# Norming block 1 of sequence 0 by the common path, and moving three loads of x behind a later norm

## The chip, the cores and the metric

One core of one Trainium2 chip. The metric is the device time of one execution in microseconds (us): before the change the median of 3 runs is 859.71 us (859.6 to 859.87). The engines are TensorE (PE; its weight loads are shown apart as PEld), VectorE (DVE), ScalarE (ACT), GpSimd (POOL) and SyncE (SP). SP only issues transfers, and GpSimd issues some as well.

## The reference

Eight sequences of 3008 rows and 256 columns are filtered along the rows in the frequency domain. Each row of the result is then normed, and goes through a gated feed-forward layer of width 1536.

```python
X = np.fft.rfft(x, axis=1)
Y = X * (filt_r + 1j * filt_i)[None, :, :]
y = np.fft.irfft(Y, n=x.shape[1], axis=1)          # per sequence
rms = np.sqrt(np.mean(y * y, axis=-1, keepdims=True) + 1e-06)
xn = y / rms * rms_g
g = xn @ w_gate
out = (g * (1 / (1 + np.exp(-g))) * (xn @ w_val)) @ w_out
```

## The kernel before, in words

**The mixing.** 3008 is 47 times 64, so the transform is made in two steps of matmuls for each sequence. Step a (`a_unit`) takes x from a tile of `x_load` (384 KB, four for each sequence, issued by GpSimd, float32 in HBM to float16 in SBUF) and its result goes to HBM by `z_store`. `t2_load` brings it back in another layout, four loads for each sequence. Step b (`b_unit`, or `b_soft`) is a matmul, followed by the product with the filter (`s_part`, `add_unit`). A transposing transfer (`yt_load`), step bi (`bi_unit`) and four transposing transfers (`t4_load`) follow. All transfers but the loads of x and of the weights are issued by SP.

**The norm.** The output rows come in six blocks of four tiles (m = 0 to 5) for each sequence. `norm_plan` gives a block to the common path: `n_unit` twice (one matmul of 512 columns into the PSUM bank "mx", and its copy to the float32 tile y by ACT), `sq_unit` twice (two squares with their sums on ACT), `stat_unit` (u and rho, the mean and its power of -1/2, on GpSimd), `xt_unit` (y times rho on GpSimd) and `tr_unit` (a transposing transfer on SP, from xt to xn). Block 0 of sequence 0 has its own path, `first_norm`. Block 1 of sequence 0 has another one: `n_first` (eight matmuls of 128 columns, two squares and two copies on ACT), `q_unit` (eight matmuls that sum the squares, u on DVE, rho on GpSimd), `scale_split` (two small operations on DVE) and `scale_apply` (eight matmuls that spread rho over the partitions, and two products on DVE that write xn). It uses no transfer.

**The feed-forward layer.** `items` lists 576 slots (b, m, jt): eight sequences, six blocks, twelve slices of the width. In slot i the program issues `gv` (four matmuls of 512 columns, lines 553, into the banks pg and pv, two buffers each; then Silu on ACT, L557, and the product on DVE, L558), then the planned steps of that slot in the order of a list, then `down` for slot i - 2 (four matmuls of 256 columns, L578). Slot 12 is the first that reads xn of block 1, slot 24 the first that reads xn of block 2.

**What sets the order.** Each engine runs its instructions in the order of the program. `fit` finds a slot for a step by a load that it counts for each engine and bank ("A" ACT, "V" DVE, "M" and "B" the banks "mx" and "mb"), and `at` puts the step into the plan of that slot. `XAT` holds the earliest slots of the loads of x: (6, 8, 11, 29) for sequence 2. Transfers that SP issues run on one queue, in the profile q1, and those of GpSimd on another, q0. Both are served by the core's 16 DMA engines.

Around the change the plan of before is: slot 2 the first `z_store` of sequence 1; slot 3 `n_first`; slot 5 `q_unit` (behind `down`); slot 7 `scale_split`; slot 9 `scale_apply`; slots 5 to 11 the eight `a_unit` of sequence 1 that are left, all with their copies on ACT; slots 6, 8 and 11 three loads of x of sequence 2; slots 7, 9 and 12 the other three `z_store`; slots 12 to 20 the norm of block 2 (`stat_unit` in 16, `xt_unit` in 17, `tr_unit` in 20); slots 15, 16, 17 and 25 the `t2_load` of sequence 1; slot 19 its first `b_unit`.

Of the kernel before, what the change touches and what calls it, by code (L numbers as in the profile page):

```python
# [10 lines left out]
FP32 = mybir.dt.float32  # L11
FP16 = mybir.dt.float16
AXT = mybir.ActivationFunctionType
ALU = mybir.AluOpType
# [6 lines left out]
P = 128  # L21
D = 256
B = 8
# [9 lines left out]
Y_SCALE = N * S_INV_B * S_INV_A  # L33
XC = 6
# [67 lines left out]
def kernel(  # L102
# [11 lines left out]
    nc = tc.nc  # L114
# [17 lines left out]
    xtp = ctx.enter_context(tc.tile_pool(name="xtp", bufs=2))  # L132
    up = ctx.enter_context(tc.tile_pool(name="up", bufs=2))
    xnp = ctx.enter_context(tc.tile_pool(name="xnp", bufs=4))
    hp = ctx.enter_context(tc.tile_pool(name="hp", bufs=4))
    op = ctx.enter_context(tc.tile_pool(name="op", bufs=2))
# [4 lines left out]
    psB = ctx.enter_context(tc.tile_pool(name="psB", bufs=1, space=bass.MemoryType.PSUM))  # L141

    tab = glob.tile([P, 5 * P], FP16)
    wa, wai, ident = (tab[:, ts(i, P)] for i in range(3))
# [13 lines left out]
    ones = glob.tile([P, 1], FP16)  # L158
    epsb = glob.tile([P, 1], FP32)
    warm = glob.tile([P, 4], FP32)  # L160
    mhalf = glob.tile([P, 4], FP32)
    seen = glob.tile([P, 4], FP16)

    st = {b: {"x": {}, "t1": {}, "t2": {}, "s": {}, "yt": {}, "t4": {}, "y": {}, "sq": {},
              "u": {}, "xn": {}} for b in range(B)}
# [4 lines left out]
    def y_tile():  # L170
        t = stg.tile([P, 2, 4, 256], FP32, tag="stg", name="y")
        return t.rearrange("p a b c -> p (a b c)")[:, 0:1024].rearrange("p (a e) -> p a e", a=2)
# [16 lines left out]
    def bank(i, name):  # L189
        pool, tag = ((psM, "mx"), (psG, "pg"), (psV, "pv"), (psB, "mb"), (psO, "po0"))[i]  # L190
        return pool.tile([P, 512], FP32, tag=tag, name=name)

    def copy(eng, out, in_, scale=None):
        if eng == "A":
            nc.scalar.activation(out=out, in_=in_, func=AXT.Copy, **({} if scale is None else {"scale": scale}))  # L195
        elif scale is None:
            nc.vector.tensor_copy(out=out, in_=in_)
        else:
            nc.vector.tensor_scalar(out=out, in0=in_, scalar1=scale, scalar2=None, op0=ALU.mult)
# [277 lines left out]
        nc.scalar.activation(out=warm, in_=mhalf, func=AXT.Silu)  # L477
        st[0]["xn"][0] = xn

    def n_first(m):  # L480
        y = y_tile()
        sq = xtp.tile([P, 4, D], FP16, tag="xt", name="sq").rearrange("p (a e) d -> p a (e d)", a=2)
        psn = [bank((0, 3)[h], "psn") for h in range(2)]
        for h in range(2):
            for q in (2 * h, 2 * h + 1):
                n1p = 4 * m + q
                src = st[0]["t4"][n1p // XC][:, n1p % XC]
                for dh in range(2):
                    nc.tensor.matmul(psn[h][:, ts(2 * (q % 2) + dh, P)], src[:, ds(dh * P, P)], wai,
                                     start=True, stop=True)  # L490
        for h in range(2):
            nc.scalar.activation(out=sq[:, h, :], in_=psn[h], func=AXT.Square)
        for h in range(2):
            copy("A", y[:, h, :], psn[h])
        st[0]["sq"][m] = sq
        st[0]["y"][m] = y

    def q_unit(m):
        sq = st[0]["sq"].pop(m)
        ps = psB.tile([P, 4], FP32, tag="mb", name="psq")  # L500
        for q in range(4):
            for dh in range(2):
                nc.tensor.matmul(ps[:, q:q + 1], sq[:, q // 2, ts(2 * (q % 2) + dh, P)], ones,
                                 start=(dh == 0), stop=(dh == 1))
        u = up.tile([P, 4], FP32, tag="u", name="u")
        rho = up.tile([P, 4], FP32, tag="rho", name="rho")
        nc.vector.tensor_scalar(out=u, in0=ps, scalar1=1.0 / D, scalar2=1e-6 * Y_SCALE * Y_SCALE,
                                op0=ALU.mult, op1=ALU.add)
        nc.gpsimd.tensor_tensor(out=rho, in0=u, in1=mhalf, op=ALU.pow)
        st[0]["u"][m] = rho  # L510

    def scale_split(m):
        rho = st[0]["u"].pop(m)
        hl = up.tile([P, 2, 4], FP16, tag="hl", name="hl")
        nc.vector.tensor_copy(out=hl[:, 0, :], in_=rho)
        nc.vector.tensor_tensor(out=hl[:, 1, :], in0=rho, in1=hl[:, 0, :], op=ALU.subtract)
        st[0]["u"][m] = hl

    def scale_apply(m, bk):
        hl = st[0]["u"].pop(m)  # L520
        y = st[0]["y"].pop(m)
        ps = bank(bk, "psr")
        for q in range(4):
            for e in range(2):
                nc.tensor.matmul(ps[:, ts(q, P)], hl[:, e, q:q + 1].to_broadcast([P, P]), ident,
                                 start=(e == 0), stop=(e == 1))
        xn = xnp.tile([P, 4, 2, P], FP16, tag="xn", name="xn")
        pv = ps.rearrange("p (q t) -> p q t", q=4)
        for h in range(2):
            nc.vector.tensor_tensor(out=xn[:, 2 * h:2 * h + 2],  # L530
                                    in0=pv[:, 2 * h:2 * h + 2].unsqueeze(2).to_broadcast([P, 2, 2, P]),
                                    in1=y[:, h, :].rearrange("p (q e t) -> p q e t", q=2, e=2), op=ALU.mult)
        st[0]["xn"][m] = xn

    LAST = (B - 1, 5)
    hh_of = {}
    po_of = {}
# [92 lines left out]
    with tc.manual_schedule():  # L630
# [48 lines left out]
        todo = [(i, f, dh) for i in range(2) for f in range(2) for dh in range(2)][:7] + [(2, 0, 0)]  # L679
# [58 lines left out]
        a_out(1, 2, "V", ahead[0])  # L738

        items = [(b, m, jt) for b in range(B) for m in range(6) for jt in range(JT)]  # L740
        plan, late = {}, {}
        front = (sq_unit, s_part, add_unit)
        load = {r: [0.0] * (len(items) + 99) for r in "MBAV"}
        room = {"A": 0.8, "V": 0.7}
# [2 lines left out]
            load["V"][i] = 0.68  # L747

        def at(slot, fn, *a):
            todo = (late if fn == q_unit else plan).setdefault(slot, [])  # L750
            if fn in front:
                todo.insert(0, (fn, a))
            else:
                todo.append((fn, a))
# [20 lines left out]
        def norm_plan(b, m, slots, r):  # L775
            for i in range(2):
                s = fit(slots[i], ("M", 0, 1), ("A", 0, 0.6), ("A", 1, 0.82))
                at(s, n_unit, b, m, i)
                at(s + 1, sq_unit, b, m, i)
            for d, fn in zip(r, (stat_unit, xt_unit, tr_unit)):  # L780
                at(s + d, fn, b, m)
            assert s + r[-1] + 1 < 72 * b + 12 * m

        def a_plan(b, slots):
            for i in range(4 * (b == 1), 12):
                opts = []
                for k in "MB":
                    opts.append((k, "A", ((k, 0, 1), ("A", 0, 0.6))))
                    opts.append((k, "V", ((k, 0, 1), (k, 1, 1), ("V", 0, 0.68))))
                k, e, need = min(opts, key=lambda o: fit(slots[i], *o[2], keep=False))  # L790
                s = fit(slots[i], *need)
                at(s, a_unit, b, i, e, 0 if k == 'M' else 3)
                if i % 3 == 2:
                    at(s + 1, z_store, b, i // 3)
                    if b + 1 < B:
                        at(max(s + 2, XAT.get(b + 1, (0,) * 4)[i // 3]), x_load, b + 1, i // 3)
            return s + 1
# [20 lines left out]
                        at(last, bi_unit, b, u)  # L818
            return last

        XAT = {2: (6, 8, 11, 29), 3: (47, 51, 79, 88), 4: (112, 122, 132, 142)}
        at(0, a_out, 1, 3, "A", ahead[1])
        at(2, z_store, 1, 0)
        at(XAT[2][0], x_load, 2, 0)
        at(3, n_first, 1)
        at(5, q_unit, 1)
        at(7, scale_split, 1)
        at(9, scale_apply, 1, 3)
        load["M"][3] = load["M"][4] = 1
        load["B"][3] = load["B"][4] = load["B"][5] = load["B"][9] = load["B"][10] = 1  # L830
        load["A"][3] = load["A"][4] = 1.2
        for m, n_at in ((2, 12), (3, 20), (4, 31), (5, 42)):
            norm_plan(0, m, (n_at, n_at + 2), (2, 3, 6))
        for b in range(1, B):
            t = (b - 1) * 72
# [43 lines left out]
        for i in range(len(items) + 4):  # L879
            for fn, a in early.pop(i, ()):  # L880
                fn(*a)
            if i < len(items):
                gv(*items[i])
            for fn, a in plan.pop(i, ()):
                fn(*a)
            if 2 <= i < len(items) + 2:
                b, m, jt = items[i - 2]
                if jt == 1 and i > JT:
                    down(b, m, 0)
                if jt or i < JT:  # L890
                    down(b, m, jt)
                if items[i - 2][2] == JT - 1:
                    stores[i + 1] = items[i - 2][:2]
            for fn, a in late.pop(i, ()):
                fn(*a)
            if i in stores:
                o_store(*stores[i])
        assert not plan and not late and not early


# [28 lines left out]
```

## Time and profile before

| what | value |
|---|---|
| median of 3 runs | 859.71 us |
| the profiled execution, its own time | 859.65 us |
| its span, first to last instruction | 857.9 us |
| what lies around the span | 1.75 us |
| granted TensorE clock | 1.000 |
| PE busy | 849.2 us (99%), 6139 matmuls |
| DVE busy | 557.2 us (65%) |
| ACT busy | 612.5 us (71%) |
| POOL busy | 298.1 us (35%) |
| DMA packets of q1 (SP), of q0 (GpSimd) | 189464 (85.52 MB), 8544 (21.24 MB) |

The page's busy time of PE is not work at its peak, since matmuls are pipelined. What a stretch costs is read from the distance between the starts of the same matmul in successive slots. The slots begin at 43.20 us of the span (slot 0) and the last matmul ends at 853.6 us.

### The profile page before, as it was taken

How to read it: one execution, taken by the hardware profiler on the slowest of the kernel's cores; microseconds unless marked ns; L12 is line 12 of the kernel's file. 1: busy time of each engine (PE TensorE's matmuls, PEld its weight loads, DVE VectorE, ACT ScalarE, POOL GpSimd, SP SyncE). 2: the span in 40 equal slices, each digit the busy share in tenths (PEclk: the TensorE clock that was granted, in tenths of full speed). 3: DMA queues.
4: the chain of work that ended last, by engine and by line, in shares of the span. 5: the costliest groups of instructions: out<-in, count | busy, mean ns of one | idle time of the engine just before them, and what ended most of it. 6: DMA issues, size and time to landing. Idle time of an engine off the chain costs nothing.

```text
span 857.9 us, 17015 instructions
## 1 busy us (share of the span) xinstructions
PE 849.2 (99%) x6139; PEld 532.5 (62%) x6139; DVE 557.2 (65%) x926; ACT 612.5 (71%) x1338; POOL 298.1 (35%) x346
## 2 busy tenths in 40 slices
PE   8999999999999999999999999999999999999997
PEld 6766666666666666666666666666666666665655
DVE  5857755776666666666666676767666665555554
ACT  4987887786687757887578865887567765777444
POOL 5725732543154413443044430444123430132000
PEclk9999999999999999999999999999999999999999
DMA  9995878756975566746747658434574431521101
GB/s 282 273 206 126 152 169 168 148 123 137 186 138 140 108 142 114 158 117 129 152 122 115 120 108 185 105 81 113 122 126 93 98 69 42 123 56 50 63 25 50
DMA packets 198237, 107.98 MB, mean 126 GB/s; under 512 B 158566, under 2 KB 182520, under 8 KB 198152
## 3 DMA queue, kind: packets, MB, share of 16 engines
q1 hardware_dynamic: 189464, 85.52, 44.9%
q0 software_dynamic: 8544, 21.24, 12.9%
q8 instruction: 48, 0.79, 0.4%
q14 instruction: 37, 0.30, 0.1%
q10 hardware_dynamic: 144, 0.13, 0.0%
HBM read 45.78 MB, written 35.65 MB: 95 GB/s over the span
## 4 chain that ended last, share of the span: by engine, by line
PE 97%; DMA 1%; DVE 0%; ACT 0%; POOL 0%; issue 0%; DVEq 0%; POOLq 0%
PE po L578 29%; PE pg L553 28%; PE pv L553 28%; PE psb L248 3%; PE psi L292 3%; PE psn L321 2%; PE psa L204 2%; DMA fs<-in_filt_i_dram 1%; PE psy L425 1%; PE psf L396 1%; PE pst L374 0%; POOL xc L186 0%; DVE s L238 0%; ACT ff L195 0%; ACT sq L455 0%
## 5 line engine op out<-in xcount | busy, mean ns | idle before, releaser
L558 DVE TENSOR_TENSOR hh<-pv,sg 128x512 f16<-128x512 f32 (+1 forms) x577 | 391.6, 679 | 283.4 <-ACT sg L557 220.5
L557 ACT ACTIVATE sg<-pg 128x512 f16<-128x512 f32 (+1 forms) x577 | 337.5, 585 | 215.2 <-PE pg L553 211.4
L553 PE MATMUL pg<-xn,wg 128*128 128x512 f16 (+2 forms) x1156 | 337.9, 374 | 0.0
L553 PE MATMUL pv<-xn,wv 128*128 128x512 f16 (+2 forms) x1156 | 337.8, 374 | 0.0
L578 PE MATMUL po<-wo,hh 128*128 128x256 f16 x2256 | 332.7, 272 | 0.0
L578 PEld LDWEIGHTS <-hh 128*128 128x128 f16 x2256 | 213.4, 98 | 105.2
L275 POOL TENSOR_TENSOR ss<-s,s 128x384 f16<-128x384 f16 x112 | 102.0, 912 | 267.4 <-DVE s L241 239.8
L553 PEld LDWEIGHTS <-wv 128*128 128x128 f16 x1156 | 113.0, 98 | 130.6 <-issue 0.2
L553 PEld LDWEIGHTS <-wg 128*128 128x128 f16 x1156 | 111.5, 98 | 16.9 <-issue 0.2
L347 POOL TENSOR_TENSOR xt<-y,rho 128x1024 f16<-128x1024 f32 (+1 forms) x46 | 85.4, 1857 | 2.9
L329 ACT ACTIVATE junk<-y 128x256 f16<-128x256 f32 x180 | 74.3, 413 | 2.8
L238 DVE TENSOR_TENSOR s<-psb,ff 128x384 f16<-128x384 f32 x124 | 67.8, 548 | 0.7 <-ACT ff L195 0.6
L241 DVE TENSOR_TENSOR s<-psb,ff 128x384 f16<-128x384 f32 x124 | 67.7, 547 | 0.0
L195 ACT ACTIVATE uu<-psi 128x384 f16<-128x384 f32 (+1 forms) x127 | 61.8, 487 | 1.1
L195 ACT ACTIVATE y<-psn 128x512 f32<-128x512 f32 (+1 forms) x95 | 55.7, 588 | 4.2
L292 PEld LDWEIGHTS <-yt 96*128 96x128 f16 x512 | 35.5, 97 | 26.2 <-issue 0.2
L339 POOL TENSOR_TENSOR rho<-u,mhalf 128x4 f32<-128x4 f32 (+1 forms) x46 | 46.5, 1011 | 3.8
L337 POOL TENSOR_SCALAR u<-ss 128x4 f32<-128x4 f32 (+1 forms) x46 | 8.9, 194 | 106.4 <-ACT junk L329 105.4
L195 ACT ACTIVATE t<-psa 128x512 f16<-128x512 f32 x70 | 41.4, 595 | 2.8 <-PE psa L204 1.4
L292 PE MATMUL psi<-wi,yt 96*128 96x96 f16 x512 | 42.9, 205 | 0.0
L248 PE MATMUL psb<-wb,t 96*128 96x96 f16 x480 | 40.0, 206 | 0.0
L248 PEld LDWEIGHTS <-t 96*128 96x128 f16 x480 | 29.3, 97 | 10.7 <-issue 0.2
(102 smaller groups left out, 364.2 us busy)
## 6 DMA issues: line engine op xcount, KB each, us to landing
out_dram<-o SPq DMA_DIRECT2D x40, 512.0 KB, 3.5
xc<-in_x_dram POOLq DMA_DIRECT2D x31, 384.0 KB, 6.1
z_tmp<-t SPq DMA_DIRECT2D x28, 384.0 KB, 2.7
t<-z_tmp SPq DMA_DIRECT2D x28, 384.0 KB, 6.0
out_dram<-o SPq DMA_DIRECT2D x7, 384.0 KB, 2.7
fs<-in_filt_i_dram POOLq DMA_DIRECT2D x3, 512.0 KB, 10.8
fs<-in_filt_r_dram POOLq DMA_DIRECT2D x3, 512.0 KB, 11.3
ws<-in_moe_w_gate_dram POOLq DMA_DIRECT2D x3, 512.0 KB, 10.0
```

The lines of the kernel that those rows point to most:

```text
L195: nc.scalar.activation(out=out, in_=in_, func=AXT.Copy, **({} if scale is None else {"scale": scale}))
L238: eng.tensor_tensor(out=o, in0=ps, in1=f1, op=ALU.mult)
L241: eng.tensor_tensor(out=o, in0=ps[:, :, ::-1, :], in1=f2, op=ALU.mult)
L248: nc.tensor.matmul(ps[:, ts(k, KR)], st[b]["t2"][kk // KC][:, kk % KC, ds(dh * P, P)], wb[0:KR, kk, :], start=True, stop=True)
L275: nc.gpsimd.tensor_tensor(out=ss3[g % 3][:, :, dh, 0:KR], in0=s[0], in1=s[1], op=ALU.add)
L292: nc.tensor.matmul(ps[:, k, :], yt[0:KR, k, dh, :], wi[0:KR, 4 * g + k, :], start=True, stop=True)
L329: nc.scalar.activation(out=junk, in_=y[:, i, ts(u, D)], func=AXT.Square, accum_out=ss[:, 2 * i + u:2 * i + u + 1])
L347: nc.gpsimd.tensor_tensor(out=xt[:, 0:n, :], in0=y.rearrange("p a (u d) -> p (a u) d", u=2)[:, 0:n, :], in1=rho[:, 0:n].unsqueeze(2).to_br ...
L553: nc.tensor.matmul(ps[:, (r0 - q0) * P:(r1 - q0) * P], wt[:, dt_, ts(jt, P)], xn[:, r0:r1, dt_, :], start=(dt_ == 0), stop=(dt_ == 1))
L557: nc.scalar.activation(out=sg[:, c], in_=pg[:, 0:w], func=AXT.Silu)
L558: nc.vector.tensor_tensor(out=hh[:, c], in0=pv[:, 0:w], in1=sg[:, c], op=ALU.mult)
L578: nc.tensor.matmul(po[q - 1][:, 0, :] if own else po[q // 2][:, q % 2, :], hh_of[(b, m, j)][:, ts(q, P)], wo[:, j, :], start=(j == 0 and ( ...
```

## The change

Block 1 of sequence 0 goes to the common path, with `n_unit` in slots 2 and 3, `stat_unit` in slot 5, `xt_unit` in slot 6 and `tr_unit` in slot 8. Its own functions are removed. `fit` then places the steps a of sequence 1 otherwise: unit 4 in slot 4 with its copy on DVE, and one unit in each of the slots 5 to 11, with copies on ACT. The second `z_store` of sequence 1 is put into slot 9 (before: 7). The three loads of x move from the slots 6, 8 and 11 to 17, 18 and 20. In GpSimd's order the first one stands between `stat_unit` and `xt_unit` of block 2, the other two directly behind `xt_unit` of block 2. In SP's order `tr_unit` of block 1 stands between the first and the second `z_store`. From slot 21 on both plans are the same, step for step.

```diff
-    def n_first(m):
-        y = y_tile()
-        sq = xtp.tile([P, 4, D], FP16, tag="xt", name="sq").rearrange("p (a e) d -> p a (e d)", a=2)
...
-    def q_unit(m):
...
-    def scale_split(m):
...
-    def scale_apply(m, bk):
...
-        plan, late = {}, {}
+        plan = {}
...
-            todo = (late if fn == q_unit else plan).setdefault(slot, [])
+            todo = plan.setdefault(slot, [])
...
-                    at(s + 1, z_store, b, i // 3)
+                    at(9 if (b, i) == (1, 5) else s + 1, z_store, b, i // 3)
...
-        XAT = {2: (6, 8, 11, 29), 3: (47, 51, 79, 88), 4: (112, 122, 132, 142)}
+        XAT = {2: (17, 18, 20, 29), 3: (47, 51, 79, 88), 4: (112, 122, 132, 142)}
         at(0, a_out, 1, 3, "A", ahead[1])
         at(2, z_store, 1, 0)
         at(XAT[2][0], x_load, 2, 0)
-        at(3, n_first, 1)
-        at(5, q_unit, 1)
-        at(7, scale_split, 1)
-        at(9, scale_apply, 1, 3)
-        load["M"][3] = load["M"][4] = 1
-        load["B"][3] = load["B"][4] = load["B"][5] = load["B"][9] = load["B"][10] = 1
-        load["A"][3] = load["A"][4] = 1.2
+        norm_plan(0, 1, (2, 3), (2, 3, 5))
         for m, n_at in ((2, 12), (3, 20), (4, 31), (5, 42)):
             norm_plan(0, m, (n_at, n_at + 2), (2, 3, 6))
...
-            for fn, a in late.pop(i, ()):
-                fn(*a)
```

More of the change, by code (lines that the diff above doesn't have):

```diff
@@ L478, in first_norm @@
         st[0]["xn"][0] = xn
-    def n_first(m):
-        y = y_tile()
-        sq = xtp.tile([P, 4, D], FP16, tag="xt", name="sq").rearrange("p (a e) d -> p a (e d)", a=2)
[L483 to L496, printed above, removed]
@@ L498, in q_unit @@
-    def q_unit(m):
[L499 to L510, printed above, removed]
@@ L512, in scale_split @@
-    def scale_split(m):
[L513 to L517, printed above, removed]
-    def scale_apply(m, bk):
[L520 to L533, printed above, removed]
@@ L893 @@
                     stores[i + 1] = items[i - 2][:2]
-            for fn, a in late.pop(i, ()):
-                fn(*a)
             if i in stores:
                 o_store(*stores[i])
-        assert not plan and not late and not early
+        assert not plan and not early
 _INS = ['x', 'filt_r', 'filt_i', 'moe_w_gate', 'moe_w_val', 'moe_w_out', 'moe_rms_g']
```

## The prediction

> **What bounds the kernel now.** I read the page first, then the chain, then the timeline of slots 0 to 26, then the DMA windows.
>
> ```profile
> PE 849.2 (99%) x6139; PEld 532.5 (62%) x6139; DVE 557.2 (65%) x926; ACT 612.5 (71%) x1338; POOL 298.1 (35%) x346
> PE 97%; DMA 1%; DVE 0%; ACT 0%; POOL 0%; issue 0%; DVEq 0%; POOLq 0%
> ```
>
> The chain that ended last is TensorE nearly everywhere. In the table by stages TensorE is busy without a break from 60 us on, and its waits add up to a few us, all before slot 0. So a matmul that goes is a gain, and any wait of TensorE is a loss that nothing later gives back.
>
> **Matmuls removed and added.** Distances between the starts of successive pg pairs (TensorE in the timeline) give the price of a step:
>
> ```profile
> 46.44 0.59 PE L553 MATMUL pg<-xn,wg 128*128 128x512 f16 x2
> ...
> 47.30 0.61 PE L489 MATMUL psn<-tab,t 128*128 128x128 f16 x8
> ...
> 49.48 0.59 PE L553 MATMUL pg<-xn,wg 128*128 128x512 f16 x2
> ```
>
> Slot 4 starts at 48.18 and has no extra step: 49.48 - 48.18 = 1.30 is a plain slot. Slot 3 with `n_first` takes 48.18 - 46.44 = 1.74, so `n_first` costs 0.44. Slot 7 with one `a_unit` takes 1.52 (52.93 to 54.45), so 0.22 for one matmul of 512. Slot 5 with `a_unit` and `q_unit` takes 1.72: `q_unit` 0.20. Slot 9 with `a_unit` and `scale_apply` takes 1.96 (55.96 to 57.92): 0.44. Removed: 0.44 + 0.20 + 0.44 = 1.08. Added: two matmuls of `n_unit`, 0.22 each as in slot 12 (60.95 to 62.47, 1.52): 0.44. The eight `a_unit` of slots 5 to 11 are still eight. **Sum: -0.64 us**, 0.07% of the run. What else decides is whether something new makes TensorE wait.
>
> **Block 1's own path, slots 2 to 12.** ACT loses two squares and two copies (1.08 + 1.09) and one `a_unit` copy (0.60, now 0.69 on DVE, which loses five operations of block 1). It gains two copies (0.60) and two `sq_unit`, which take 0.94 each where they stand elsewhere (63.60 to 64.54). Followed in ACT's order: copy at 46.4, Silu of slot 3 at 47.3, copy at 47.9, squares at 48.5, Silu of slot 4 at 49.45, squares until 51.05, Silu of slot 5 until 51.5. The pg buffer of slot 5 is wanted again at 52.7, that of slot 4 at 51.2 (free at 50.0), so the backlog costs TensorE nothing; if it grew by 1.2 us, it would cost what is above that. GpSimd then does as for block 2 (below): 3.4 us from the end of the squares to the end of xt, so 54.45, and SP issues the transfer there. At that moment the load of x issued at 46.98 has just landed (54.8), no other is queued, since the three of sequence 2 have gone, and the first `z_store` lands at 55.1. Transposing transfers beside stores alone took 3.1 to 4.8 us, so xn lands at 57.5 to 59.3; slot 12 starts at 60.95 - 0.64 = 60.3. Hidden, with 1 us to spare at least. The z stores queued on SP behind this wait go out at about 55.8 in place of 53.1, and the last still leaves near 60.7; their first reader, the `t2_load` behind the store of the output, issues at 65.4. Hidden too.
>
> **The moved loads, slots 17 to 24.** From here I use the clock of before; TensorE, GpSimd and SP all come 0.64 earlier together. GpSimd:
>
> ```profile
> 67.61 0.19 POOL L337 TENSOR_SCALAR u<-ss 128x4 f32<-128x4 f32 x1 [11.04 <-ACT junk L329]
> 67.90 1.04 POOL L339 TENSOR_TENSOR rho<-u,mhalf 128x4 f32<-128x4 f32 x1
> 69.02 1.89 POOL L347 TENSOR_TENSOR xt<-y,rho 128x1024 f16<-128x1024 f32 x1
> ```
>
> SP, and the matmul of slot 24 that needs the xn of this xt:
>
> ```profile
> 66.06 2.25 SPq L228 DMA_DIRECT2D t<-z_tmp  x3
> 70.94 1.26 SPq L356 DMA_TRANSPOSE xn<-xt  x1
> ```
>
> ```profile
> 78.11 0.59 PE L553 MATMUL pg<-xn,wg 128*128 128x512 f16 x2
> ```
>
> In before, three loads of t are on q1 when the transpose is issued at 70.94; it lands 3.6 us later, at 74.55, with 3.5 us to spare. After the change GpSimd issues the first load of x at 68.95 (the end of rho), which takes 0.6 us of GpSimd, so xt ends 0.6 later, at 71.5. There the transpose is issued, and the other two loads in the same 1.2 us. `add_unit`, next on GpSimd, waits for DVE until 73.4 anyway. So three loads of x (q0) meet two loads of t and the transpose (q1), on the same 16 engines. How q0 and q1 share is seen where a load of x met a transpose, at 390 to 391 us:
>
> ```profile
> q0 software_dynamic: 59, 0.18, 93.4%
> q1 hardware_dynamic: 58, 0.01, 11.2%
> ```
>
> The columns are packets, MB and share of the engines. One for one by packets: 3072 bytes of x for each 256 of the transpose. So the transpose hardly moves until the load is through. That load and that transpose, issued within 0.1 us, landed after
>
> ```profile
> xc<-in_x_dram POOLq DMA_DIRECT2D x1, 384.0 KB, 5.2
> xn<-xt SPq DMA_TRANSPOSE x1, 5.9
> ```
>
> [...]
>
> Since q1 is in order and the transpose is its last, it lands when all that work is done. Terms: one load of x alone takes 4.8 us to landing (issued at 90.74), start-up included. Each further one adds 128 packets at 91 in 1.5 us (93.0 to 94.5): 2.1. A load that is issued at 68.95 shows its first packet some 1.3 us later, as that of 90.74 did, so at 70.3. From there on before still had on q1
>
> ```profile
> q1 hardware_dynamic: 2280, 0.87, 98.9%
> ```
>
> of which 1024 are the transpose's, 64 completions, and about 1190 are of t. The last go at 2103 in 4.0 us (68.5 to 72.5), so 2.3; the transpose's at 912 in 1.0 us (270 to 271), so 1.1. Landing: 68.95 + 4.8 + 2 x 2.1 + 2.3 + 1.1 = **81.35**. The same sum for collisions in before comes out at 393.2 (load of 387.29; measured 393.3), 271.5 (265.63; 271.6), 179.9 (172.97, with a store of 1.1; 180.2), 472.7 (466.77; 473.9) and 124.4 (115.31, two loads and a store; 125.8): 0.1 to 1.4 too early, median 0.3. I take 81.6. Slot 24 waits from 78.1 to 81.6: **+3.5 us**. The bounds: 80.6 if the 24 t packets per engine that go between those of x are free (0.7 less), 83 with the largest miss: a wait of 2.5 to 5.
>
> The first load of t, needed by slot 19's `b_unit` at 71.14 and landed at 70.73, has its last packets at 69.8, 0.5 before those of x. Should x catch it, part of the wait moves to slot 19, and the sum stays. The second is read behind slot 24's wait, the third in slot 30; x itself in slot 29, at 85.4. After the wait both plans are equal, and TensorE alone sets the pace.
>
> **Forecast.** 859.65 - 0.64 + 3.5 = 862.5 for an execution like the profiled one; the median of the runs shown lies 0.06 above it, so **862.6**. Its own range is 861.6 to 864.1 (waits of 2.5 to 5).
>
> **Rivals.**
>
> *B, not slower: the queues share engine time, not packets.* Then q1's 3.4 us of work from 70.3 on, after a start-up of 0.8, take twice as long at most: 70.3 + 0.8 + 6.8 + 0.5 for landing = 78.4, a wait of 0.3. It decides at a landing of 78.1. The time is 859.71 - 0.64 + 0.3 = 859.4, or 859.1 without a wait. For it: packets of t (512 bytes) beside x are in no row. Against it: 59 to 58. Chance 0.14.
>
> *C, between them:* the start-up of x doesn't stop q1, or x comes later, and the wait is 0.5 to 2.3: 859.6 to 861.4. Against it: 387 to 389 us, where q1 fell from some 400 packets in half a us to none. Chance 0.10.
>
> *D, the clock falls in the wait.* The kernel's first ten fills (L433, from 1.45 us) take 4.0 us, four later ones 1.0: a cold TensorE runs at about half rate. A wait of 3.5 us is longer than any gap of TensorE in before since the first matmul (0.8). If it brings that state back for 3 to 4 us, 1.7 to 2 more are lost: 864.3 to 864.6, and up to 866 with a long wait. [...] Chance 0.09.
>
> *E, block 1 is late as well.* Its transpose would have to take the 7.1 us of the row at 466.77: landing at 61.6, slot 12 waits 1.3, 863.9. Against it: no load of x is beside it. Chance 0.07.
>
> *The change doesn't do what it says:* the first load does stand behind the statistics of block 2, but ahead of its xt; that is what I priced.
>
> **Chances.** The forecast's case has 0.60. Without B the range would hold about 0.75, so it reaches down to B and leaves out most of D: 859.0 to 864.6. Some 0.2% (1.7 us) is what a measurement here can tell from no change. Faster by more than that needs a gain that no row has: 0.01. Within it are B and C: 0.23. Slower: 0.76.
>
> **What would show it.** In the profile after: psq, psr and `hl` gone and slots 3 to 9 shorter (else the -0.64 is wrong); a wait of TensorE at L553's successor in slot 24, by a DMA xn<-xt, of some 3.5 us; that transpose at about 10 us to landing; x loads of q0 one for one with q1 between 69.7 and 77; none of TensorE in slot 12. If the transpose of block 2 lands in under 6.5 us, the sharing was read wrongly, and the time is near 859.1.

## The result and the profile after

After the change the median is 862.77 us (861.18 to 863.05, 8 executions), before it 859.75 us (859.48 to 860.35, 8 executions). The ratio is 1.003, with a 95% interval of 1.0019 to 1.0041: slower by 3.0 us. The prediction was 862.6, in a range of 859.0 to 864.6.

The 8 executions lie on two levels, and each has its mean granted clock of TensorE (1.000 is full speed): 861.18, 861.32 and 861.88 us at 1.000, and five from 862.71 to 863.05 at 0.997 or 0.998. The profiled execution is on the lower level (861.32 us, span 859.5 us). So two things need an answer: where 861.32 comes from, and what adds some 1.5 us in most executions.

The lines behind the functions of block 1, which are gone, have moved by 55: L498 is the old L553 (`gv`), L523 the old L578 (`down`). The page of after has, for busy time and chain:

```profile
PE 849.1 (99%) x6117; PEld 531.7 (62%) x6117; DVE 556.4 (65%) x922; ACT 612.9 (71%) x1343; POOL 299.9 (35%) x348
PE 96%; DMA 2%; POOL 1%; DVE 0%; ACT 0%; issue 0%; DVEq 0%; POOLq 0%
```

There are 22 matmuls less, and a share of the chain has gone from TensorE to transfers and GpSimd. TensorE's waits in after (us in total, times, longest) begin with one that before does not have:

```profile
PE pg L498 <- DMA xn<-xt: 2.2, 1, 2.2
```

The timeline of TensorE in after, slots 3 and 4 and the start of slot 12, then the start and the end of slot 23 and slot 24:

```profile
46.60 0.59 PE L498 MATMUL pg<-xn,wg 128*128 128x512 f16 x2
...
47.47 0.38 PE L321 MATMUL psn<-t,tab 128*128 128x512 f16 x1
...
48.12 0.59 PE L498 MATMUL pg<-xn,wg 128*128 128x512 f16 x2
...
60.25 0.59 PE L498 MATMUL pg<-xn,wg 128*128 128x512 f16 x2
```

```profile
75.76 0.59 PE L498 MATMUL pg<-xn,wg 128*128 128x512 f16 x2
...
76.96 0.60 PE L523 MATMUL po<-wo,hh 128*128 128x256 f16 x4
79.73 0.59 PE L498 MATMUL pg<-xn,wg 128*128 128x512 f16 x2 [2.17 <-DMA xn<-xt]
```

In before, the slots 12 and 23 start here:

```profile
60.95 0.59 PE L553 MATMUL pg<-xn,wg 128*128 128x512 f16 x2
...
76.47 0.59 PE L553 MATMUL pg<-xn,wg 128*128 128x512 f16 x2
```

Slot 3 takes 1.52 in place of 1.74. Slot 12 starts at 60.25 in place of 60.95, of which 0.05 was there at slot 0 already: 0.65 saved. Slot 23 takes 3.97 us (75.76 to 79.73) in place of 1.64 (76.47 to 78.11): 2.33 lost. Then -0.05 - 0.65 + 2.33 = +1.63, and the spans differ by 859.5 - 857.9 = 1.6. Behind slot 24 the matmuls gain another 0.1 and the end of the program takes 0.15 longer; nothing else in the profiled execution differs.

GpSimd and SP in after, around the norm of block 2:

```profile
67.18 1.01 POOL L339 TENSOR_TENSOR rho<-u,mhalf 128x4 f32<-128x4 f32 x1
68.15 0.64 POOL L186 DMA_DIRECT2D xc<-in_x_dram  x1
68.81 1.91 POOL L347 TENSOR_TENSOR xt<-y,rho 128x1024 f16<-128x1024 f32 x1
70.65 1.24 POOL L186 DMA_DIRECT2D xc<-in_x_dram  x2
```

```profile
65.35 2.21 SPq L228 DMA_DIRECT2D t<-z_tmp  x3
70.75 1.26 SPq L356 DMA_TRANSPOSE xn<-xt  x1
```

The chain of after crosses exactly here (start, us, what):

```profile
68.81 1.92 POOL xt L347
70.73 0.02 issue
70.75 8.94 DMA xn<-xt
```

Before, the same transpose took 3.6 us. The DMA windows of after tell what it waited for. From 68.15, when the first load of x is issued, to 72.0 only q1 moves; from 72.6 to 74.0 only q0; from 75 to 76 both; from 78.5 to 79.5 only q1 (packets, MB, share of the engines):

```profile
q1 hardware_dynamic: 1907, 0.96, 120.9%
```

```profile
q0 software_dynamic: 102, 0.30, 108.9%
```

```profile
q0 software_dynamic: 66, 0.19, 95.9%
q1 hardware_dynamic: 66, 0.02, 12.5%
```

```profile
q1 hardware_dynamic: 975, 0.24, 125.6%
```

So the loads of t go through untouched. The first load of x then has the engines for itself, and the transpose, whose issue came at 70.75, does not move. From 74.5 on it goes one packet for one of the second and third load, and runs free only when these are through.

### The profile page after: what moved, and what is told of

It reads as the page before. It is cut to its first block, busy times and chain, and to the rows that moved or that the text cites. A ratio compares the mean times of both kernels' runs of the same rounds, so it can differ in the third digit from the quotient of the medians.

```text
span 859.5 us, 16981 instructions
## 1 busy us (share of the span) xinstructions
PE 849.1 (99%) x6117; PEld 531.7 (62%) x6117; DVE 556.4 (65%) x922; ACT 612.9 (71%) x1343; POOL 299.9 (35%) x348
## 4 chain that ended last, share of the span: by engine, by line
PE 96%; DMA 2%; POOL 1%; DVE 0%; ACT 0%; issue 0%; DVEq 0%; POOLq 0%
PE po L523 28%; PE pg L498 28%; PE pv L498 28%; PE psb L248 3%; PE psi L292 3%; PE psn L321 2%; PE psa L204 2%; DMA fs<-in_filt_i_dram 1%; DMA xn<-xt 1%; PE psy L425 1%; PE psf L396 1%; PE pst L374 0%; POOL xc L186 0%; POOL xt L347 0%; DVE s L238 0%
## 5 line engine op out<-in xcount | busy, mean ns | idle before, releaser
L498 PE MATMUL pg<-xn,wg 128*128 128x512 f16 (+2 forms) x1156 | 337.9, 374 | 2.2 <-DMA xn<-xt 2.2
L498 PE MATMUL pv<-xn,wv 128*128 128x512 f16 (+2 forms) x1156 | 337.8, 374 | 0.0
L523 PE MATMUL po<-wo,hh 128*128 128x256 f16 x2256 | 332.6, 272 | 0.0
L523 PEld LDWEIGHTS <-hh 128*128 128x128 f16 x2256 | 213.5, 98 | 105.5
L498 PEld LDWEIGHTS <-wv 128*128 128x128 f16 x1156 | 113.0, 98 | 130.6 <-issue 0.2
L498 PEld LDWEIGHTS <-wg 128*128 128x128 f16 x1156 | 111.6, 98 | 19.1 <-issue 2.5
L347 POOL TENSOR_TENSOR xt<-y,rho 128x1024 f16<-128x1024 f32 (+1 forms) x47 | 87.3, 1857 | 2.9
```

What stands on the lines that cost most here:

```text
L347: nc.gpsimd.tensor_tensor(out=xt[:, 0:n, :], in0=y.rearrange("p a (u d) -> p (a u) d", u=2)[:, 0:n, :], in1=rho[:, 0:n].unsqueeze(2).to_br ...
L498: nc.tensor.matmul(ps[:, (r0 - q0) * P:(r1 - q0) * P], wt[:, dt_, ts(jt, P)], xn[:, r0:r1, dt_, :], start=(dt_ == 0), stop=(dt_ == 1))
L523: nc.tensor.matmul(po[q - 1][:, 0, :] if own else po[q // 2][:, q % 2, :], hh_of[(b, m, j)][:, ts(q, P)], wo[:, j, :], start=(j == 0 and ( ...
```

## The experiments

Theory 1: the loads of x ahead of the transpose make slot 24 wait; block 1's common path itself only saves matmuls. Theory 2: the upper level comes from TensorE's clock, which drops in that wait or just behind it.

**loads_only**, the moved loads without block 1's new path:

```diff
 (before)
-        XAT = {2: (6, 8, 11, 29), 3: (47, 51, 79, 88), 4: (112, 122, 132, 142)}
+        XAT = {2: (17, 18, 20, 29), 3: (47, 51, 79, 88), 4: (112, 122, 132, 142)}
```

> Before, with nothing but the three loads of x moved to the slots 17, 18 and 20; block 1 keeps its own path. Theory 1 (the loads ahead of the transpose of block 2 make slot 24 wait 2.2 us; where the clock drops as well, 1.6 us more): 859.75 + 2.2 = 862.0, up to 863.6 with a clock of 0.997, and a wait of some 2.2 us for xn in slot 24. Rival (the loss comes from block 1's common path, its squares on ACT or its transfer on SP): 859.75, no wait.

Measured: 864.06 us against 859.78 of before on that chip, ratio 1.0045 (1.0031 to 1.0058). One of the 4 executions, the profiled one, took 862.17 (clock 0.999), the others 864.01 to 864.37 (0.997 and 0.998). Its waits have

```profile
PE pg L553 <- DMA xn<-xt: 2.5, 1, 2.5
```

The moved loads do it alone. The lower level is as expected; the upper lies 0.4 to 0.8 above what I gave.

**loads_late**, all three loads behind the transpose:

```diff
 (after)
-        XAT = {2: (17, 18, 20, 29), 3: (47, 51, 79, 88), 4: (112, 122, 132, 142)}
+        XAT = {2: (21, 22, 23, 29), 3: (47, 51, 79, 88), 4: (112, 122, 132, 142)}
```

> After, with the three loads in the slots 21, 22 and 23, so that GpSimd issues them behind the next add_unit and the transpose of block 2 is already out. Theory 1: no wait in slot 24, clock 1.000, and the matmuls saved are what is left: 859.75 - 0.65 = 859.1. Rival (block 1's common path costs): 861 to 863 as in after.

Measured: 859.26 us (859.10 to 859.46, 11 executions, all at 0.999 or 1.000), ratio 0.9993 (0.9985 to 1.0002). The profile has no wait for xn. The common path of block 1 costs nothing. That it gains its 0.65 is seen in the slots, and the medians differ by 0.52, but the interval holds 1.

**one_ahead**, XAT (17, 21, 22, 29), one load ahead:

> After, with one load ahead of the transpose (slot 17) and the other two in 21 and 22. Theory 1 with a price of 2.0 us for each load ahead: the transpose lands 4.0 us earlier than in after, at 75.7 against a need at 77.4 (slot 24): no wait, 859.1. Rival (a single load ahead, with its start-up, holds the transpose nearly as long as three): a wait of 1 us or more, 860 and up.

Measured: 859.20 us (859.05 to 859.90, 10 executions), ratio 0.9994 (0.9985 to 1.0003), no wait for xn. One load ahead is hidden.

**two_ahead**, XAT (17, 18, 21, 29):

> After, with two loads ahead of the transpose and the third behind the next add_unit (XAT 17, 18, 21). Theory 1: the transpose of block 2 lands 2.0 us earlier than in after, at 77.7 against a need at 77.4: a wait of 0.3 us, 859.4, clock 1.000. Rival (a threshold rather than a price for each load): the wait of after, 861.3 and up.

Measured: 859.40 us; nine of 10 executions from 858.99 to 859.69, one at 868.06 with a clock of 0.995 for which I have no profile; ratio 1.0006 (0.9987 to 1.0024). The timeline of TensorE in its slot 24:

```profile
77.80 0.59 PE L498 MATMUL pg<-xn,wg 128*128 128x512 f16 x2 [0.23 <-DMA xn<-xt]
```

Slot 23 takes 2.04 us, 0.40 more than in before; 0.3 was expected. So each load has a price, and there is no threshold between two and three. What made the one execution of 868.06 slow stays open.

**four_ahead**, XAT (17, 18, 20, 20):

> After, with the fourth load of x of sequence 2 issued with the other three (XAT 17, 18, 20, 20). Theory 1 at 2.0 us for each load ahead: a wait of 2.2 + 2.0 = 4.2 us in slot 24, 861.3 + 2.0 = 863.3. Theory 2 (the clock drops in a long wait, 1.6 us): 864.9 in nearly all executions, clock 0.997, and the drop to be seen in the profile behind slot 24. Rival (the wait is set by something else than the number of loads): 861.3 to 862.8 as in after.

Measured: 865.44 us (864.90 to 865.87, 4 executions, clock 0.995 to 0.997), ratio 1.0066 (1.0052 to 1.008). Slot 23 loses 0.40, 2.33 and 4.18 us (5.82 against 1.64) with two, three and four loads ahead: 1.9 us for the third and for the fourth. This profile has the drop of the clock. The table by stages, cut at the edges where the granted clock changes (us of the stretch, busy time of PE, PEld, DVE, ACT and POOL with counts, PEclk, DMA share, GB/s):

```profile
75.70:79.12 3.42, 1.86 (x19) 1.17 (x17) 1.70 (x3) 2.29 (x7) 1.65 (x2) 1.00 1.08 206
79.12:82.53 3.41, 0.95 (x7) 0.48 (x7) 0.00 (x0) 0.33 (x1) 3.18 (x5) 1.00 1.20 245
82.53:85.94 3.41, 3.41 (x17) 1.83 (x16) 2.49 (x5) 0.91 (x3) 2.03 (x3) 0.50 0.35 61
85.94:89.35 3.41, 3.41 (x25) 2.09 (x24) 3.04 (x6) 1.75 (x3) 2.13 (x3) 1.00 0.75 203
```

Its timeline has the pairs of matmuls at two speeds, in slots 24 and 25:

```profile
81.58 0.59 PE L498 MATMUL pg<-xn,wg 128*128 128x512 f16 x2 [4.01 <-DMA xn<-xt]
...
83.52 1.06 PE L498 MATMUL pg<-xn,wg 128*128 128x512 f16 x2
```

TensorE has been back at work for one us when the clock falls to half, and it stays there for 3.41 us, which loses 1.7. In after's profile, on the lower level, the stretch with most of the wait, cut by the same step of 3.41 us from that profile's own start of the clock, had

```profile
77.84:81.26 3.42, 1.53 (x13) 1.00 (x13) 0.61 (x2) 1.06 (x3) 2.80 (x3) 1.00 1.19 243
```

and no drop behind it. So a stretch with 28% of busy TensorE brought the drop, and one with 45% did not.

The other profiles narrow this down. Each was cut by 3.41 us from its own first record of the clock, and the end of the program, where TensorE runs out of work, gives such stretches too: in before the clock is 0.50 from 858.21, in after from 859.49, both behind a stretch without a matmul, and both 853.33 us behind the first record (4.88 and 6.16), which is 250 steps of 3.413. That the stretches follow one another by this step throughout is my reading of these edges. From four_ahead behind its last matmul, from loads_only around its wait of 2.5 us, and from block1_only (below) in its wait of 5.1 us:

```profile
857.35:860.76 3.41, 1.36 (x13) 0.88 (x10) 1.40 (x4) 0.80 (x2) 0.00 (x0) 1.00 0.25 91
76.66:80.07 3.41, 1.52 (x16) 0.96 (x15) 1.36 (x3) 1.96 (x7) 1.67 (x3) 1.00 1.12 198
61.67:65.09 3.42, 0.00 (x0) 0.00 (x0) 0.00 (x0) 0.00 (x0) 0.00 (x0) 1.00 1.23 114
```

The clock was 0.50 behind the first and the third, and 1.00 behind the second. In all ten profiles every stretch with up to 1.36 us of busy TensorE is followed by the drop, and none with 1.52 or more. So in these profiles the drop came where TensorE stood idle for 2.05 us or more of one stretch (3.41 - 1.36), and not where it did for 1.9 or less (3.41 - 1.52). My estimate from these numbers is that after's gap of 2.17 us brings it in about half of its possible positions, and one of 4.0 us practically always; five of 8 and four of 4 executions had it. The drops behind the last matmul cost nothing. In four_ahead that one begins at 860.76 of a span of 863.1, and 2.3 us at half the clock take 0.0014 off the mean; by this estimate it can be why executions without a drop in the work show 0.999 as well as 1.000.

**filled**, work for TensorE in the wait. Nothing reads the result of these matmuls:

```diff
 (after)
+            if i == 24:
+                pf = bank(3, "pf")
+                for _ in range(9):
+                    nc.tensor.matmul(pf, wa, tab[:, 0:512], start=True, stop=True)
             if i < len(items):
                 gv(*items[i])
```

> After, with nine matmuls of 512 columns on tables put ahead of the matmuls of slot 24 (1.95 us of work that nothing reads), so that TensorE is busy during most of the wait. Theory 2 (the second level of times near 862.8 is the clock that drops in the wait): every execution at 861.3, clock 1.000. Rival (the wait itself has two lengths, by how the transfers meet): still two levels, 861.3 and 862.8.

Measured: 862.00 us, one level, 861.71 to 862.44 in 9 executions, clock 0.999 or 1.000; ratio 1.0026 (1.0016 to 1.0036). The matmuls had to wait 0.8 us for ACT, which still read their bank, so that slot 24 starts at 80.88, 0.7 us after the transpose had landed (80.13); that is why the level is 862.0 and not 861.3.

**filled2**, the same with two matmuls in place of nine:

> The kernel 'filled' with two of the nine matmuls (0.43 us of work in a wait of 2.2 us, at about 0.8 us from its start). Theory 2a (the clock drops only when TensorE stands still for most of two us on end): one level of times at 861.3, clock 0.999 or 1.000 throughout. Theory 2b (it is the sum of idle time in a stretch that counts): two levels as in after, 861.3 and 862.8.

Measured: 861.33 us, 861.10 to 862.04 in 11 executions, clock 0.999 or 1.000; ratio 1.0019 (1.001 to 1.0028). Slot 24 starts at 79.72, where it starts in after (79.73):

```profile
78.31 0.59 PE L824 MATMUL pf<-tab 128*128 128x512 f16 x2 [0.78 <-ACT y L264]
79.72 0.59 PE L498 MATMUL pg<-xn,wg 128*128 128x512 f16 x2 [0.82 <-DMA xn<-xt]
```

Two useless matmuls in the wait make the kernel 1.4 us faster than after, since the clock then stays up: two gaps of 0.78 and 0.82 us leave 2.61 us of work in each of the two stretches that they touch. There is one level of times in both runs, so the upper level of after is the clock (theory 2) and not a second length of the wait (the rival). Whether the longest gap or the sum of idle time in a stretch decides is not settled, since 0.4 us of work changes both.

**block1_only**, XAT (6, 8, 11, 29) in after, the loads where before has them:

> After, with the loads where before has them (XAT 6, 8, 11): block 1's common path alone. GpSimd then issues the first load ahead of xt of block 1 and the other two right behind it, so they meet the transpose of block 1. By 2.0 us for each load ahead the transpose lands near 60 against a need at 60.25 in slot 12: a wait of 0 to 0.5, 859.1 to 859.6. Rival (the loads cost there what they cost in slot 24): a wait of 2 us in slot 12, 861.3, and more where the clock drops.

Measured: 867.31 us (863.68 to 869.41, 4 executions, clock 0.993 to 0.998), ratio 1.0088 (1.0061 to 1.0114), with

```profile
PE pg L498 <- DMA xn<-xt: 5.1, 1, 5.1
```

in slot 12. Both expectations fell short. The clock is at 0.50 from 65.09 to 68.50, behind the idle stretch shown above; by half of the 2.96 us in which TensorE works there, this costs another 1.5. From 57.5 to 59 us the transpose went one for one with the second load (73 packets of q1, 81 of q0), but then, from 60.3 to 62.0, hardly anything moved on either queue:

```profile
q1 hardware_dynamic: 180, 0.05, 134.3%
q0 software_dynamic: 7, 0.02, 12.3%
```

180 packets in 1.7 us where 975 went in one, and each of them long: by the share of the engines some 0.2 us against 0.02. This was beside the start of the third load, which had been issued at 55.80. What made them long is not known. The run does show that in this plan, with the loads at their old place, the common path costs far more than it saves.

## Why the prediction was right, and where only by luck

*Matmuls, -0.64:* measured -0.65.

*Block 1's path hidden:* right. Slot 12 waits for nothing, and rival E, a late block 1, did not come.

*The moved loads delay the transpose of block 2, and slot 24 waits:* right in place, cause and sign (loads_only, loads_late, and two, three and four loads ahead).

*The size, "Slot 24 waits from 78.1 to 81.6: +3.5 us":* this step failed. The loss in slot 23 is 2.33 us. The mis-sized term is the 4.8 us of the first load. I counted from its issue 1.3 us to the first packet, some 0.8 until packets flow, and put the rest of t behind both. In after the load's packets begin at 72.1 and flow at once, because t was served to its end first: what was start-up, the 0.8 too, lay beside t. Then I added 0.3 for misses of the sum in cases where the engines had stood idle before the load. In the clock of after: the first load until 74.4; two more beside the transpose, 256 packets at 66 in a us, 3.9 us; the transpose's other 631 packets (393 had gone beside the loads) at some 1000 in a us, 0.6; landing 0.7. That gives 79.6; the chain has 70.75 + 8.94 = 79.69. My other terms were off by less than 0.5 each and nearly cancel (t longer, two loads and transpose shorter).

*One for one by packets:* right for the second and third load (66 against 66), wrong for the first, which neither let t wait nor let the transpose in. For the end of the work the order of sharing mattered little, since all of it had to be through; the start-up did.

*Rival C, 0.10:* this is what the profiled execution did. C had the start-up of x not stop q1, or x come later, with a wait of 0.5 to 2.3 and 859.6 to 861.4. The wait is 2.2 and the time 861.32, with t untouched until 72.1; my own case had waits of 2.5 to 5. I held C small by the row at 387 to 389 us, where q1 did stop (402 packets from 387.5 to 388, none from 388.5 to 389). Before's trace had a row for the other side: GpSimd issues a load of weights at 46.19, and from 46.20 to 48.90 all 1823 packets are of q1.

*Rival D, the clock, 0.09:* with C, this is what I weighed worst. It came in five of 8 executions, in a wait of 2.2 us and not 3.5, and it cost 1.5 us. The 3 to 4 us at half rate that I assumed had nothing behind them but the first ten fills (4.0 us), and no run then showed such a state behind a wait (before has the clock at 0.50 only behind its last matmul, from 858.21). In four_ahead and block1_only the clock was at 0.50 for 3.41 us, behind stretches in which TensorE was busy for 0.95 us and not at all; up to 1.36 us were seen. The 0.09 was my estimate and rested on no measured case.

So 862.6 agrees with the median by luck. It stands on two errors of opposite sign: a wait too long by 1.2 us and a clock drop of 1.5 us left out. What came was C and, in five of 8 executions, D on top of it. The profiled execution alone, 861.32, was predicted as 862.5. The signs that I named, a wait of "some 3.5 us" and a transpose of "about 10 us", were 2.2 and 8.9 in the profile.

*Rival B, not slower:* refuted. The transpose landed 2.3 us behind its need.

## What to carry to other kernels

A transfer that is moved to a quiet place for one block is at once beside the next block's transfers; look for what lands latest in the new place, and count how many loads are queued ahead of it. Here one ahead was free, the second used up the slack and cost 0.4 us, and the third and fourth cost 1.9 us each. Where a change makes TensorE wait about as long as here, look at the granted clock of every execution: the wait of 2.2 us was paid a second time, by some 1.5 us, in five of 8 executions of after, and two useless matmuls in it saved that part in all 11 executions of filled2.

## What the runs showed of the hardware that I had not expected

- A load of x issued by GpSimd while three loads of t were on SP's queue sent no packet for 3.9 us (68.15 to 72.1), although the one at 90.74 in before needs 1.3. The transpose issued at 70.75 in turn sent none until that load was through (74.5). Where packets alternated one for one in after (66 and 66, 75 to 76 us), both sides had been waiting when the engines came free; that this is the condition is not shown, and the mechanism is not known.
- The clock of TensorE dropped to 0.50 behind stretches of 3.41 us in which it was busy for 0 to 1.36 us, and not behind those with 1.52 us or more, in all ten profiles; with work behind it, in four_ahead and block1_only, it stayed there for 3.41 us. In four_ahead the drop came one us after work had begun again, in block1_only 0.45 us before (65.09 against 65.54): in both it came at the edge of the stretch, not at a fixed time from the wait.
